# One remainder step of the angle changes places with k's product with the decay, from unit 3 on

## The chip, the cores and the metric

The kernel runs on one core of a Trainium2 chip. The metric is the device time of one execution in microseconds. A core has five engines that work side by side, each through its own instructions in order: TensorE (PE, with its weight loads as PEld), VectorE (DVE), ScalarE (ACT), GpSimd (POOL) and SyncE (SP), of which SP here only issues DMAs.

## The reference

An attention block with complex gates is followed by a gated feed-forward block. Sizes: 4 batches, 8 heads, 768 steps of time, head width 48; 3072 tokens, model width 384, inner width 1024.

```python
scale = np.minimum(mag, 0.999) / (mag + 1e-06)      # mag = |a_re + i a_im|
...
for t in range(S):
    new_re = ar * S_re - ai * S_im
    new_im = ar * S_im + ai * S_re
    S_re, S_im = (new_re + kv, new_im)              # kv = outer product of k and v at t
    y[:, :, t] = np.einsum('bhd,bhde->bhe', q[:, :, t], S_re)
...
h = ((x @ w1) * (x @ w2)) @ w3
return h @ w_out                                    # x is y with the heads side by side
```

## The kernel before

**Units.** A unit is half of one batch's time: 384 steps of all 8 heads, so there are 8 units, 0 to 7. The channels lie as 3 column tiles of 384 steps on 128 partitions. The recurrence is not stepped: the gates are brought to a running decay and a running angle, k and q are multiplied by decay (or its inverse), cosine and sine, and then scores, states and outputs are matrix products (lines 997 to 1081). Behind a unit's outputs come the feed-forward products of that unit, w1 and w2 (lines 1083 to 1136, `m` in the trace) and the fused w3 times w_out (lines 1178 to 1193, `o`).

**Feed-forward products from unit 3 on.** Each of the 16 column blocks of w1 and w2 takes a first product of six matmuls (called h0, h1, ... in the prediction), a copy of its PSUM tile in place by ScalarE (L1125), and a correction of three matmuls onto the same tile (d0, d1, ...). An even correction is followed by a copy to `ab` by ScalarE (L1132), an odd one by a product into `ab` by VectorE (L1107). There are four PSUM banks for them (`ps_m`), and the order on TensorE is h0, h1, h2, d0, h3, d1, h4, d2, and so on. So h4 takes the bank of h0, once the copy behind d0 has ended. Each `o` product is cut into two halves of eight matmuls; ScalarE copies the result behind the second (L1190). Of the products of unit u - 1 some stand ahead of the transposes, scores and outputs of unit u, and the last of them, two halves or three of the `o` products, behind them.

**Gates.** While TensorE works on the products of unit u - 1, VectorE and ScalarE prepare unit u in `gates_apart` (lines 624 to 769), in two parts: part 0 is column tile 0 (128x384), part 1 is tiles 1 and 2 (128x768). A step on a part has its number behind its name. The steps that matter here, in the order of the program:
- `ang_0`, `ang_1` (L687, VectorE): running sums of the angle, one per tile; `turns_0`, `turns_1` (L691, ScalarE): the whole turns in it as integers; a small copy of the angles (L692, VectorE).
- `k_0`, `k_1` (`scaled`, L703, VectorE): k times the inverse decay. It needs k from memory.
- `z5_0` (L709, VectorE): the angle of tile 0 less its whole turns; `abs_0`, `cos_0` (L711, L713, ScalarE); then `z5_1`, `abs_1`, `cos_1`.
- `q_0`, `q_1` (L717, VectorE), `sin_0`, `sin_1` (L723, ScalarE), the end columns (L729, ScalarE, three small copies).
- `kc`, `qc`, `ks`, `qs` (L749, L752, L757, L763, VectorE): k and q times cosine and sine, each followed by DMAs on SP's queue that lay the tiles out for the scores (L739), and at last the DMAs of V (L592).

ScalarE's steps that go through the helper `act` all bear L637 in the trace. k, q and V of unit u + 1 are loaded by GpSimd's queue (L528, L570) when the outputs of unit u have been written, behind the last GpSimd step of these outputs (L1053).

**Who sets the order.** TensorE's order is a list written ahead (`unit`, `pieces`, `ffn`). The order of all other engines comes from a planner that runs while the program is built (`run`, lines 1576 to 1737): it keeps a clock per engine from the costs written in `TIMES` and in the `yield`s, and behind every item of TensorE's list it takes the next gate step if that step can start before TensorE is through the next item (`fits`, `fill`). Gate steps are taken strictly in the order of the generator; the next is looked at only when the one before has been placed. So a gate step's place in its engine's queue is a place between the copies of two products. A ScalarE step of n tiles is written as 0.2 + 0.325 n, a VectorE one as 0.06 + 0.475 n, a first product as 1.05, a correction as 0.53, a half as 2.58, a hand-over as 0.15; a copy behind a product as 0.48 on ScalarE and 0.56 on VectorE.

```python
bound = clock["PE"] + sum(d for kind, _ in seq[k + 1:k + 2] for e, d in TIMES[kind] if e == "PE")
slack = EARLY if k < heads[0] else LATE if gate["u"] <= held["unit"] else SLACK
return start(op) < bound and start(op) + op[1] <= request(op[0], k) + slack
```

k's landing is due in the plan at the end of the outputs plus 1.1 (GpSimd's last step), 0.7 (issue), 1.8 and 2.4 (transfer) and 0.2 (lines 560 to 563, 1724).

Of the kernel before, what the change touches and what calls it, by code (L numbers as in the profile page):

```python
# [378 lines left out]
def kernel(  # L379
# [244 lines left out]
    def gates_apart(u, A, Z):  # L624
# [7 lines left out]
        def on(e, name, i, *after):  # L632
            n = (1, KD - 1)[i]
            return e, (0.2 + 0.325 * n if e == "ACT" else 0.06 + 0.475 * n), (name, i), after

        def act(**kw):
            chain(nc.scalar.activation(**kw))  # L637
# [61 lines left out]
        def scaled():  # L699
            for i, s in parts:  # L700
                yield on("DVE", "k_", i, ("r2_", i), ("k", u))
                k = g["k"][:, :, 0:TT]
                tt(out=k[:, s], in0=k[:, s], in1=r[:, s], op=OP.mult)  # L703

        if u > 2:
            yield from scaled()
        for i, s in parts:
            yield on("DVE", "z5_", i, ("turns_", i))
            stt(out=Z[:, s], in0=re[:, s].bitcast(I32), scalar=-2 * PI, in1=Z[:, s], op0=OP.mult, op1=OP.add)  # L709
            yield on("ACT", "abs_", i, ("z5_", i))  # L710
            act(out=re[:, s], in_=Z[:, s], func=AF.Abs)  # L711
            yield on("ACT", "cos_", i, ("abs_", i))
            act(out=re[:, s], in_=re[:, s], func=AF.Sin, scale=-1.0, bias=QUARTER)  # L713
# [57 lines left out]
    def gates(u, split):  # L771
# [18 lines left out]
        if u > 1:  # L790
            yield from gates_apart(u, A, Z)
            return
# [1051 lines left out]
```

## Time and profile before

| | us |
|---|---|
| median of 3 runs | 538.68 |
| lowest and highest run | 535.29, 539.11 |
| the profiled execution | 539.2 |
| its span in the profile | 537.4 |

The profile is that of one execution. Its span reaches from the first instruction to the last; 1.8 us of the execution lie around it. A timeline row has the start, the time, the engine and line, what is written from what, the shape and the count, and in brackets the engine's idle time just before with what ended it. A row of waits has the sum, the count and the longest. PE rows of the products overlap each other by some tenths, since matmuls are pipelined.

### The profile page before, as it was taken

The page shows a single profiled execution, that of the slowest core. Times are in us where ns is not written, and L with a number is a line of the kernel's source. Part 1 is how long each engine was busy: PE and PEld are TensorE (multiplying, and loading weights), DVE is VectorE, ACT ScalarE, POOL GpSimd, SP SyncE. Part 2 cuts the span into 40 slices and gives each one's busy share as a digit, 9 for nine tenths or more (in the row PEclk, how much of TensorE's full clock was granted, in tenths as well). Part 3 has the DMA queues.
Part 4 walks back from the last instruction along what each step waited for, and adds up shares of the span by engine and source line. Part 5 has one row for each costly group of instructions (what it writes and reads, how often), then busy time and mean ns, then how long its engine had stood idle before and what let it go on. Part 6 is the DMA issues. An engine that isn't in the chain of part 4 may idle for free.

```text
span 537.4 us, 13665 instructions
## 1 busy us (share of the span) xinstructions
PE 498.4 (93%) x5594; PEld 377.7 (70%) x5594; DVE 374.0 (70%) x607; ACT 336.8 (63%) x569; POOL 247.1 (46%) x311
## 2 busy tenths in 40 slices
PE   4689889999998999999999999999999999999995
PEld 2355565556755678967888678867996788878972
DVE  6999697856769977866873776578657846336660
ACT  6979867485575556884788457855797555213420
POOL 1000000017868866830675565576458458335510
PEclk9899899999999999999999999999999999999999
DMA  8999966874178616494569437972797166935511
GB/s 249 367 395 280 189 200 176 227 171 111 40 204 212 116 57 187 116 224 80 141 195 224 93 77 204 227 138 63 197 214 135 46 176 167 213 95 187 194 56 37
DMA packets 66520, 89.75 MB, mean 167 GB/s; under 512 B 29968, under 2 KB 53968, under 8 KB 65680
## 3 DMA queue, kind: packets, MB, share of 16 engines
q1 hardware_dynamic: 58016, 59.15, 44.0%
q0 software_dynamic: 8432, 29.63, 20.2%
q8 instruction: 46, 0.75, 0.6%
q14 instruction: 26, 0.21, 0.1%
HBM read 61.60 MB, written 4.72 MB: 123 GB/s over the span
## 4 chain that ended last, share of the span: by engine, by line
PE 48%; DVE 16%; DMA 16%; issue 6%; ACT 5%; POOL 5%; SPq 2%; POOLq 0%; DVEq 0%; ACTq 0%
PE m L1091 21%; PE o L1186 16%; PE y L1045 5%; PE sc L1006 4%; DMA k<-in_k_dram 3%; DMA V<-vr 2%; DMA QL<-gA 2%; DMA KL<-k 2%; DVE gA L752 2%; DVE gR L749 2%; DMA q<-in_q_dram 1%; DMA look<-in_a_re_dram 1%; PE kv L1071 1%; DMA raw<-in_w_dram 1%; DMA KL<-gR 1%
## 5 line engine op out<-in xcount | busy, mean ns | idle before, releaser
L1186 PE MATMUL o<-w3o,ab 128*128 128x384 f32 x384 | 131.5, 492 | 0.0
L1091 PE MATMUL m<-x,low 128*128 128x384 f32 x576 | 119.2, 339 | 0.0
L1091 PEld LDWEIGHTS m<-x,low 128*128 128x128 f32 x576 | 102.6, 188 | 0.2 <-ACT m L1125 0.2
L1186 PEld LDWEIGHTS o<-w3o,ab 128*128 128x128 f32 x384 | 70.5, 190 | 45.5 <-issue 2.2
L1107 DVE TENSOR_TENSOR ab<-m,ab 128x384 f32<-128x384 f32 x64 | 35.0, 554 | 59.3 <-PE m L1091 43.9
L1091 PE MATMUL m<-x,wh 128*128 128x384 f32 x288 | 69.8, 351 | 3.5 <-ACT ab L1132 2.5
L1125 ACT ACTIVATE m<-m 128x384 f32<-128x384 f32 x96 | 45.5, 475 | 32.7 <-PE m L1091 31.2
L1091 PE MATMUL m<-xT,ws 128*128 128x384 f32 x192 | 63.1, 487 | 1.2 <-ACT xT L1056 1.2
L1091 PEld LDWEIGHTS m<-x,wh 128*128 128x128 f32 x288 | 50.7, 188 | 7.9 <-ACT ab L1132 3.8
L1327 POOL TENSOR_SCALAR look<-look 128x192 f32<-128x192 f32 (+1 forms) x54 | 53.8, 996 | 4.9
L1091 PEld LDWEIGHTS m<-xT,ws 128*128 128x128 f32 x192 | 36.0, 190 | 25.6 <-ACT xT L1056 1.7
L1272 POOL MEMSET seen<- 128x256 bf16 x1 | 0.3, 316 | 111.8 <-DVE ab L1107 111.8
L1324 POOL TENSOR_TENSOR look<-look 128x256 f32<-128x256 f32 (+1 forms) x42 | 30.6, 730 | 43.5 <-DMA look<-in_w_dram 24.3
L1009 DVE COPY_PREDICATED A<-mask,sc 128x512 f32<-128x512 uint8 x48 | 32.8, 732 | 23.4 <-PE sc L1006 23.3
L1053 POOL TENSOR_TENSOR x<-x,x 128x384 fp32r<-128x384 f32 x18 | 22.2, 1233 | 54.4 <-DVE x L1052 54.4
L1288 POOL TENSOR_TENSOR seen<-seen,look 128x192 bf16<-128x192 bf16 (+1 forms) x54 | 43.3, 803 | 4.4
L1190 ACT COPY ot<-o 128x384 f32<-128x384 f32 x24 | 11.5, 478 | 50.5 <-PE o L1186 50.2
L1045 PE MATMUL y<-A,V 128*32 128x128 f32 x768 | 40.7, 273 | 2.5 <-issue 2.4
L994 ACT COPY KT<-tp 128x384 f32<-128x384 f32 x40 | 34.3, 867 | 6.8 <-PE tp L992 6.4
L1045 PEld LDWEIGHTS y<-A,V 128*32 128x32 f32 x768 | 34.9, 110 | 3.7 <-issue 3.2
L1006 PEld LDWEIGHTS sc<-QL,KL 96*32 96x32 f32 x1536 | 28.5, 110 | 10.3 <-issue 3.6
L1045 PE MATMUL y<-QL,T 96*32 96x128 f32 x640 | 35.3, 272 | 0.0
(163 smaller groups left out, 916.4 us busy)
## 6 DMA issues: line engine op xcount, KB each, us to landing
looked<-in_w_dram POOLq DMA_DIRECT2D x15, 512.0 KB, 4.6
look<-in_w_dram POOLq DMA_DIRECT2D x26, 256.0 KB, 4.0
raw<-in_w_dram SPq DMA_DIRECT2D x6, 1024.0 KB, 10.3
KL<-gR SPq DMA_DIRECT2D x24, 192.5 KB, 3.1
KL<-k SPq DMA_DIRECT2D x24, 192.5 KB, 7.0
QL<-gA SPq DMA_DIRECT2D x24, 192.0 KB, 9.0
QL<-q SPq DMA_DIRECT2D x24, 192.0 KB, 7.5
raw<-in_w_dram SPq DMA_DIRECT2D x6, 768.0 KB, 7.4
```

Of the source, the lines that this page charges most:

```text
L994: nc.scalar.copy(out=KT_t[u, c][:, :, :, x].rearrange("p h d f -> p f d h"), in_=tp.rearrange("p f (d h) -> p f d h", h=H))
L1006: nc.tensor.matmul(out=sc[SB * g:SB * g + SB, j, s0:C], lhsT=KL[:, x * n + j, w][:, s0:s0 + SB], rhs=QL[:, x * n + j, w][:, s0:C], start=T ...
L1009: last["sc", u, c, x] = nc.vector.copy_predicated(out=A[:, x * n:(x + 1) * n], data=sc, mask=mask)
L1045: nc.tensor.matmul(out=o, lhsT=a, rhs=b, start=s0, stop=s1)
L1053: nc.gpsimd.tensor_tensor(out=x[2], in0=x[1], in1=x[0], op=OP.subtract)
L1091: nc.tensor.matmul(out=out, lhsT=a, rhs=b, start=start and i == 0, stop=i == len(terms) - 1, skip_group_check=not start)
L1107: last["ab", u, j] = nc.vector.tensor_tensor(out=ab_t[u][:, j], in0=m, in1=ab_t[u][:, j], op=OP.mult)
L1125: nc.scalar.activation(out=got[m], in_=got[m], func=AF.Copy, scale=1.0 + 1.0 / BITS)
L1186: nc.tensor.matmul(out=m, lhsT=ab_t[u][:, f, t * P:(t + 1) * P], rhs=w3o[:, f], start=(f == 0), stop=(f == KF - 1))
L1288: nc.gpsimd.tensor_tensor(out=seen[:, 0:n], in0=seen[:, 0:n], in1=x, op=OP.add)
L1324: tt(out=x, in0=x, in1=x, op=OP.mult)
L1327: ts(out=x, in0=x, scalar1=low, scalar2=None, op0=OP.is_ge)
```

## The change

In units 3 to 7 the two instructions of `scaled` (k_0, k_1) are emitted behind the first remainder step z5_0 instead of ahead of it. The order on VectorE was k_0, k_1, z5_0, z5_1 and is written as z5_0, k_0, k_1, z5_1. In the generator abs_0 and cos_0 follow k_1 as before. Units 0 to 2 are not touched.

```diff
-        if u > 2:
-            yield from scaled()
         for i, s in parts:
             yield on("DVE", "z5_", i, ("turns_", i))
             stt(out=Z[:, s], in0=re[:, s].bitcast(I32), scalar=-2 * PI, in1=Z[:, s], op0=OP.mult, op1=OP.add)
+            if u > 2 and i == 0:
+                yield from scaled()
             yield on("ACT", "abs_", i, ("z5_", i))
             act(out=re[:, s], in_=Z[:, s], func=AF.Abs)
             yield on("ACT", "cos_", i, ("abs_", i))
```

## Rows read from the trace of the kernel before

**Rows 1.** The page's first part: busy us, share and count by engine.
```profile
PE 498.4 (93%) x5594; PEld 377.7 (70%) x5594; DVE 374.0 (70%) x607; ACT 336.8 (63%) x569; POOL 247.1 (46%) x311
```

**Rows 2.** Waits of PE over the span: who for whom, sum, times, longest.
```profile
PE m L1091 <- ACT ab L1132: 2.5, 3, 0.9
...
PE sc L1006 <- DMA V<-vr: 1.3, 1, 1.3
PE tp L992 <- DVE k L757: 1.2, 2, 0.7
...
PE m L1091 <- DVE ab L1107: 0.9, 3, 0.4
PE tp L992 <- DVE gR L749: 0.7, 3, 0.3
```

**Rows 3.** Busy time by window: width, then PE, PEld, DVE, ACT, POOL, clock, DMA.
```profile
318.00:345.00 27.00, 25.11 (x180) 22.90 (x180) 18.29 (x24) 21.11 (x40) 18.05 (x23) 1.00 0.80 206
...
430.00:462.00 32.00, 30.56 (x207) 27.42 (x206) 15.76 (x23) 18.64 (x37) 21.70 (x29) 1.00 0.73 183
462.00:537.00 75.00, 69.12 (x684) 54.08 (x682) 33.54 (x84) 16.68 (x36) 26.26 (x31) 1.00 0.41 123
```

**Rows 4.** Timeline of VectorE, gates of unit 7.
```profile
430.08 0.79 DVE L692 COPY st_ang<-gZ 128x9 f32<-128x9 f32 x1
436.55 1.43 DVE L703 TENSOR_TENSOR k<-k,gR 128x384 f32<-128x384 f32 x2 [5.68 <-DMA k<-in_k_dram]
437.89 1.43 DVE L709 SCALAR_TENSOR_TENSOR gZ<-re,gZ 128x384 f32<-128x384 int32 x2
...
446.71 0.55 DVE L749 TENSOR_TENSOR gR<-k,re 128x384 f32<-128x384 f32 x1
```

**Rows 5.** Timeline of ScalarE, gates of unit 7.
```profile
426.28 0.51 ACT L637 ACTIVATE re<-gZ 128x384 int32<-128x384 f32 x1
...
438.55 0.52 ACT L637 ACTIVATE re<-gZ 128x384 f32<-128x384 f32 x1 [1.45 <-DVE gZ L709]
438.98 0.46 ACT L1132 COPY ab<-m 128x384 f32<-128x384 f32 x1
...
439.85 0.48 ACT L1125 ACTIVATE m<-m 128x384 f32<-128x384 f32 x1
440.26 0.83 ACT L637 ACTIVATE re<-gZ 128x768 f32<-128x768 f32 x1
...
441.77 0.94 ACT L637 ACTIVATE re<-re,consts 128x768 f32<-128x768 f32 x1
```

**Rows 6.** Timeline of TensorE, units 5, 6 and 7.
```profile
325.73 0.79 PE L1091 MATMUL m<-x,wh 128*128 128x384 f32 x3 [0.82 <-ACT ab L1132]
...
382.44 0.79 PE L1091 MATMUL m<-x,wh 128*128 128x384 f32 x3 [0.85 <-ACT ab L1132]
...
427.49 0.49 PE L1045 MATMUL y<-QL,T 96*32 96x128 f32 x7
...
439.49 0.79 PE L1091 MATMUL m<-x,wh 128*128 128x384 f32 x3 [0.85 <-ACT ab L1132]
...
442.78 0.69 PE L1091 MATMUL m<-x,wh 128*128 128x384 f32 x3
```

**Rows 7.** VectorE from 300 to 450 us by form: count, busy us, mean ns.
```profile
L709 DVE SCALAR_TENSOR_TENSOR gZ<-re,gZ 128x768 f32<-128x768 int32 x3 | 2.9, 955 | 0.0
...
L709 DVE SCALAR_TENSOR_TENSOR gZ<-re,gZ 128x384 f32<-128x384 int32 x3 | 1.7, 554 | 0.0
```

**Rows 8.** Timeline of VectorE, units 3 to 6.
```profile
216.62 1.03 DVE L709 SCALAR_TENSOR_TENSOR gZ<-re,gZ 128x384 f32<-128x384 int32 x1
...
265.73 1.43 DVE L703 TENSOR_TENSOR k<-k,gR 128x384 f32<-128x384 f32 x2
...
322.85 1.43 DVE L703 TENSOR_TENSOR k<-k,gR 128x384 f32<-128x384 f32 x2 [1.13 <-DMA k<-in_k_dram]
...
377.53 1.43 DVE L703 TENSOR_TENSOR k<-k,gR 128x384 f32<-128x384 f32 x2 [1.88 <-DMA k<-in_k_dram]
```

## The prediction

> **What bounds the kernel now.** I read the page's first part, then TensorE's waits, then the busy time by stage, then the timelines of VectorE, ScalarE and TensorE around the gates of each unit from 3 on. TensorE is busy for 498.4 of 537.4 us [rows 1]: it is the bound, its order is fixed, and the change adds nothing to it and takes nothing from it. So the change is worth what it alters in TensorE's waits. From the first gates of unit 3 to the end these are few. The five groups of [rows 2] are 2.5, 1.3, 1.2, 0.9 and 0.7 us, together 6.6: the correction's copy (L1132) with three waits, V's transfer, the transposes that wait for k times sine or for k times cosine, and VectorE's products. No gain can be larger than this sum. By stage the gaps are 27.00 - 25.11 = 1.89 us in the gates of unit 5 and 32.00 - 30.56 = 1.44 in those of unit 7 [rows 3]; unit 6 has one wait of 0.85 [rows 6]. The last 75 us hold 5.9 [rows 3], about as much as the tail behind the last product needs, so a microsecond won earlier should reach the end.
>
> The three long waits have one pattern, seen best in unit 7. VectorE is done with the angle's sums and the small copy behind them at 430.87, then stands for 5.68 us until k has landed; k times decay runs from 436.55 to 437.98, and only behind it come the two remainders L709 (z5_0, z5_1) [rows 4]. ScalarE has put the turns of tile 0 down at 426.79, so z5_0 had had its input for 11 us when it started. ScalarE stands 1.45 us at the absolute value abs_0, which wants z5_0, and the correction's copy L1132 that stands behind abs_0 comes at 438.98 [rows 5]. TensorE waits for that copy for 0.85 us, until 439.49, because its fifth first product needs the PSUM bank that the copy frees; units 5 and 6 show the same with 0.82 and 0.85 [rows 6].
>
> **The change, part by part.** Nothing is added or removed: per unit one instruction of 128x384 passes two. DMA issues, SP's and POOL's queues and TensorE's order stay as they are written; what can move with them is where the planner puts the gates' later steps.
>
> *The moved instruction.* z5_0 costs 0.554 us, z5_1 0.955 [rows 7]. In units 5, 6 and 7 VectorE waits 1.13, 1.88 and 5.68 us for k [rows 4, 8], and z5_0 fits into each of these: it costs nothing there, and k's product starts when it did. If that cover were gone it would cost 0.55 us on VectorE. In units 3 and 4 VectorE doesn't wait for k (the product starts without a wait at 265.73 in unit 4) [rows 8], so there the two merely change places and z5_1 ends when it did: gain 0. From both sides: z5_0 at 1.03 (its longest, in unit 3 [rows 8]) against 0.55 could lose 0.5 us per unit, and an earlier abs_0 could win the wait for V behind unit 3, 1.3 us. I take 0, because the rest of both chains stands where it stood.
>
> The row first: z5_0 of unit 3 took 1.03 us where those of units 5 to 7 took 0.554 [rows 7, 8]. The Trainium skill, SBUF — State Buffer, section Who interferes with whom, says that a VectorE instruction with two SBUF inputs contends with a GpSimd instruction that reads SBUF, and that whichever issued later is blocked throughout. By it z5_0 of unit 5, which now starts amid GpSimd's checks, may take the longer time; the sum would be some 0.1 us less, as it would still end before k lands.
>
> *The stall that goes.* With z5_0 done before k lands, abs_0 waits for nothing. In unit 7 the copy L1132 can then run as soon as its product is there, and the 0.85 us go. What is late next is z5_1. It stands right behind k's product: 437.98 + 0.955 less some 0.1 of overlap gives 438.85, 0.3 us later than abs_0 started before (438.55 [rows 5]). So abs_1 becomes the instruction at which ScalarE stands, and all hangs on what is queued behind it.
>
> *What stands behind abs_1.* The planner decides by the costs written in the kernel; I use them for the order alone. I set its TensorE clock to 0 at the end of the last output of the unit before. Two output halves end at 5.16, then the first products h0, h1, h2 at 6.21, 7.26, 8.31, the correction d0 at 8.84, h3 at 9.89, d1 at 10.42, h4 at 11.47. k is due at 1.1 + 0.7 + 1.8 + 2.4 + 0.2 = 6.2, on VectorE it is multiplied by 7.74, z5_0 by 8.28, and abs_0 may start at 8.43: that falls behind h2's copy and ahead of d0's copy, which is where [rows 5] show it. The same walk also gives the places of cos_0, abs_1, cos_1, both sines and the end columns in the trace of before, so I trust it for after. With the change abs_0 goes behind h0's copy, cos_0 behind h1's, and abs_1 is due at 7.74 + 1.01 + 0.15 = 8.90: too late for the place ahead of d0's copy (limit 8.84), so it goes behind it and ahead of h3's. The copy that TensorE waits for is free. The end columns go from behind d5 to behind d3, and k times cosine with them, two pairs of products or about 3.2 us earlier (446.71 before [rows 4]).
>
> *Unit 5.* The same places hold, and the cosine and sine products come earlier by more than the small waits of the transposes and of L1107. All gaps of this stage go: 1.89, I take 1.9; from below 1.0, if one pair's lateness stays.
>
> *Unit 7.* abs_1 starts at 438.9. From [rows 5] a step on ScalarE costs its duration less some 0.1 of overlap: abs_1 0.73, h3's copy 0.38, cos_1 0.84, h4's copy 0.38, sin_0 0.42, d2's copy 0.36, which ends about 442.0. TensorE wants the bank that d2's copy frees at 439.49 - 0.85 + 3.2 = 441.85 (h4 to h6 is 439.49 to 442.78 [rows 6], less a slow first tile). That leaves 0.15, with the hand-over 0.3, as a new small stall. Gain 1.44 - 0.3 = 1.1.
>
> *Unit 6.* Here three halves come first, so abs_1 lands behind h0's copy and ahead of h1's, that is ahead of d0's copy too. k's product starts at 377.53 [rows 8], z5_1 ends at 377.53 + 1.43 + 0.87 = 379.83; abs_1 0.73, two copies of 0.38 and d0's 0.36 end at 381.7; TensorE begins to wait at 382.44 - 0.85 = 381.59 [rows 6]. Gain about 0.6. If the planner also puts cos_1 (0.84) ahead of d0's copy, which a few hundredths of its clock decide, the copy ends at 382.5 and 0.2 is lost. I take the middle, 0.2.
>
> *Sum.* 0 + 0 + 1.9 + 0.2 + 1.1 = 3.2 us. The profiled execution took 539.2 us, its span of 537.4 and 1.8 around it; 539.2 - 3.2 = 536.0. It lies 0.5 above the median of 538.68, so from the median I predict 535.5, 0.6% less. A measurement of this kernel can tell about 1% (5.4 us) from no change, so this would count as within it.
>
> **The rivals.**
> *A. The stall is handed on and the time stays:* abs_0 is early, but each microsecond comes back at abs_1, and the later steps keep their slots. For it: z5_1 ends as late as before, and k lands 2.4 us later than the planner thinks (436.55 is 8.6 us behind the last output's end at 427.98 [rows 4, 6], the plan has 6.2). Against it: behind h3's copy nothing urgent stands. Time 538.7, gain 0 to 1.
>
> *B. Slower: abs_1 stands ahead of d0's copy in all three units.* The point from which it decides is the planner's 8.84 for units 5 and 7; 0.06 us less in its clock is enough. Price: ScalarE goes on at z5_1's end, so d0's copy ends at z5_1's end + 0.73 + 0.36, in unit 7 at 440.0, and TensorE starts at 440.05 instead of 439.49: 0.56 worse. Unit 5 the same, unit 6 0.2: 538.7 + 1.3 = 540.0. For it: the margin is thin. Against it: the walk meets before's order everywhere.
> The Trainium skill, TensorE: Matmul & The Clock Gate, section Architectural detail: the array is 16× 32×32, not 1× 128×128, has ScalarE and VectorE as strict FIFO queues; by this rule a ready copy can't pass a waiting abs_1, and the time would be this rival's 540.0. The trace agrees that none passes: L1132 waited behind abs_0.
>
> *C. More is won:* the earlier cosine products also free the transposes of unit 4 and V's transfer behind unit 3. For it: these waits are 6.6 us in all [rows 2]. Against it: units 3 and 4 gain nothing by the steps above. 6.6 at most, 532.1.
>
> *D. The change does not do what it says:* z5_0 waits for the turns and holds k's product up. Against it: they were done long before [rows 5]. Price 0.5 a unit, 2.5: 541.2.
>
> **How the numbers follow.** Forecast (gain 2 to 4.3) 0.55; A 0.17; B 0.08; C (gain 4.3 to 6.6) 0.17; D 0.03. The range leaves out B, D and the end of C, and takes in A: 532.4 to 538.9. Faster by over 1% (under 533.3) is most of C: 0.15. Slower by over 1% (over 544.1) is beyond all priced cases: 0.03. Within 1%: 0.82.
>
> **What would show it.** Right: in units 5 to 7 z5_0 runs ahead of the wait for k, and L1132 no longer ends a TensorE wait in units 5 and 7; ScalarE's wait for L709 is now at abs_1 with 128x768; the cosine products of units 5 and 7 start 2 to 4 us earlier; the windows of units 5 and 7 lose 1 to 2 us of gaps. Wrong: the correction's copy still ends waits of 0.8 us or more in unit 5 or 7, cosine products in their old slots, or new waits of TensorE in stages where there were none.

## The result: slower, and the profile after

| | before | after |
|---|---|---|
| median of 20 runs each, us | 537.28 | 544.51 |
| the profiled execution, its span, us | 539.2, 537.4 | 546.09, 544.3 |
| ratio of the times, 95% interval | | 1.0138, 1.0115 to 1.0160 |

The changed kernel is 1.4% slower; 535.5 was forecast, with a chance of 0.03 for slower by over 1%. The page's first part and its slices of TensorE's granted clock, after (a digit is a fortieth of the span, in tenths of full speed):

```profile
PE 501.8 (92%) x5594; PEld 381.3 (70%) x5594; DVE 375.3 (69%) x607; ACT 335.5 (62%) x569; POOL 245.0 (45%) x311
...
PEclk9899899999999999999999999999889999999999
```

The same instructions, but TensorE is busy for 3.4 us more than in [rows 1], and the clock has a dip in the slices 29 and 30, about 381 to 408 us, where none was. To find the place, I cut TensorE's timeline at the end of the last output of each unit (a unit's stretch is then the feed-forward products of the unit before, with this unit's gates beside them, and its own scores and outputs):

| unit | before | after | difference | forecast |
|---|---|---|---|---|
| 3 | 56.47 | 58.61 | +2.14 | 0 |
| 4 | 57.24 | 57.18 | -0.06 | 0 |
| 5 | 54.11 | 54.41 | +0.30 | -1.9 |
| 6 | 59.63 | 67.30 | +7.67 | -0.2 |
| 7 | 53.94 | 51.94 | -2.00 | -1.1 |

With -0.86 ahead of unit 3 and -0.3 behind unit 7 that is the 6.9 us between the spans. All of it, and more, sits in unit 6. The same cut is used on the runs below. In one of their profiles, that of the change without unit 6 (e1_not6), the clock also dipped in unit 3, behind a wait of 1.52 us for V's transfer. A ratio leaves out the slow executions of a kernel (over 1.5% longer than its fastest), a median does not; the profiles of e1_not6, e2_only6 and e8_only7 are of slow ones, which are late already where unit 3 begins (205.5 to 206.8 us, before 200.5).

TensorE's waits over the span, after (who for whom, sum, times, longest):

```profile
PE m L1091 <- DVE ab L1107: 5.4, 6, 1.8
...
PE m L1091 <- ACT ab L1132: 3.5, 2, 3.2
PE sc L1006 <- DMA V<-vr: 1.6, 1, 1.6
```

Against [rows 2]: the wait for the correction's copy L1132 comes twice instead of three times, but one of the two is 3.2 us; the wait for VectorE's products L1107 has grown from 0.9 to 5.4. TensorE's timeline in units 3, 5, 6 and 7, after:

```profile
218.84 0.79 PE L1091 MATMUL m<-x,wh 128*128 128x384 f32 x3 [0.55 <-DVE ab L1107]
...
335.67 0.79 PE L1091 MATMUL m<-x,wh 128*128 128x384 f32 x3 [1.62 <-DVE ab L1107]
...
389.64 1.33 PE L1091 MATMUL m<-x,wh 128*128 128x384 f32 x3 [3.23 <-ACT ab L1132]
390.77 2.12 PE L1091 MATMUL m<-x,low 128*128 128x384 f32 x6
...
402.79 1.05 PE L1091 MATMUL m<-x,wh 128*128 128x384 f32 x3 [1.84 <-DVE ab L1107]
403.64 2.12 PE L1091 MATMUL m<-x,low 128*128 128x384 f32 x6
...
451.25 0.79 PE L1091 MATMUL m<-x,wh 128*128 128x384 f32 x3 [0.26 <-ACT ab L1132]
```

Unit 6 has two long waits, and right behind each of them six matmuls take 2.12 us. In the trace of before such six took 1.21 behind the wait of 0.85 in [rows 6]:

```profile
383.07 1.21 PE L1091 MATMUL m<-x,low 128*128 128x384 f32 x6
```

Busy time by window, after (width, then PE, PEld, DVE, ACT, POOL, clock, DMA share, GB/s):

```profile
318.00:345.00 27.00, 24.89 (x179) 22.77 (x178) 20.27 (x25) 19.89 (x39) 16.31 (x21) 1.00 0.85 210
...
372.00:402.00 30.00, 25.16 (x118) 21.44 (x116) 17.95 (x23) 19.36 (x37) 22.03 (x32) 0.94 0.61 158
...
390.00:395.00 5.00, 5.00 (x22) 5.00 (x22) 0.54 (x2) 2.95 (x9) 4.25 (x8) 0.71 0.26 73
395.00:400.00 5.00, 4.52 (x28) 4.22 (x27) 5.00 (x7) 4.05 (x7) 4.21 (x6) 1.00 0.48 133
400.00:405.00 5.00, 3.08 (x13) 2.53 (x13) 2.74 (x4) 3.31 (x6) 3.06 (x5) 0.81 0.96 206
405.00:410.00 5.00, 5.00 (x70) 4.68 (x69) 1.15 (x3) 2.98 (x6) 2.35 (x4) 0.84 1.09 237
...
402.00:430.00 28.00, 27.20 (x394) 22.02 (x395) 16.43 (x29) 18.37 (x32) 11.79 (x17) 0.94 0.67 143
```

and the same two long windows of before:

```profile
372.00:402.00 30.00, 29.15 (x200) 26.28 (x199) 17.97 (x26) 23.44 (x44) 16.91 (x24) 1.00 0.86 203
...
402.00:430.00 28.00, 27.46 (x514) 20.10 (x513) 22.06 (x34) 17.38 (x28) 17.40 (x22) 1.00 0.45 95
```

So the granted clock, 1.00 in both stretches before (the 2.4 GHz level), falls part of the time to the 1.2 GHz level: 0.71 in the window behind the first wait (0.50 from 389.6 to 392.8 us taken alone), 1.00 again from 395, 0.81 and 0.84 in the two windows with the second wait and what follows it. The 7.67 us of unit 6 come out as follows. Waits of TensorE of 0.2 us and more there: before 0.85 + 0.48 = 1.33, after 3.23 + 0.48 + 1.84 = 5.55, so 4.2 more. The rest, 3.45, is the slow clock: 58 us at 0.94 instead of 1.00 make 58 x 0.06 = 3.5.

The Trainium skill, TensorE: Matmul & The Clock Gate, section What's actually happening, says that a clock gate halves TensorE's clock when it has been idle. The trace agrees in the direction: each of the two dips stands behind a wait. Not every wait has one: behind the 1.62 us in unit 5 the clock stays at 1.00 (the window from 318 to 345 us).

What held ScalarE up? Its timeline in units 6 and 7, after:

```profile
381.27 0.85 ACT L637 ACTIVATE re<-gZ 128x768 f32<-128x768 f32 x1 [0.31 <-DVE gZ L707]
...
382.43 0.47 ACT L1132 COPY ab<-m 128x384 f32<-128x384 f32 x1
...
383.21 0.92 ACT L637 ACTIVATE re<-re,consts 128x768 f32<-128x768 f32 x1
387.46 1.25 ACT L596 ACTIVATE gA<-re,consts 128x1152 f32<-128x1152 f32 x1 [3.33 <-issue]
...
388.71 0.47 ACT L1125 ACTIVATE m<-m 128x384 f32<-128x384 f32 x1
389.12 0.47 ACT L1132 COPY ab<-m 128x384 f32<-128x384 f32 x1
...
447.93 0.85 ACT L637 ACTIVATE re<-gZ 128x768 f32<-128x768 f32 x1 [1.21 <-DVE gZ L707]
```

Up to 384.1 it goes as the better branch of the forecast has it: abs_1 waits 0.31, d0's copy at 382.43 is in time. Then comes an instruction that the prediction doesn't mention: L596, the first step of the *next* unit's gate head, a check of the sign of unit 7's `re`. It stands for 3.33 us, and behind it the copies L1125 and L1132 for which TensorE waits. The bracket names no DMA ("issue"), but the load of `re` does, by what writes that tile from 370 to 400 us:

```profile
L528 SPq DMA_DIRECT2D re<-in_a_re_dram x1: 588/588/588, 376.9 to 376.9; - x1
...
DMA to landing us min/median/max: 10.5/10.5/10.5
```

376.9 + 10.5 = 387.4: L596 starts when its input has landed. Before, it stood behind the end columns (L729), late enough:

```profile
386.35 0.20 ACT L729 COPY st_dec<-gA 128x3 f32<-128x3 f32 x1
...
387.88 1.27 ACT L596 ACTIVATE gA<-re,consts 128x1152 f32<-128x1152 f32 x1
```

The planner's rule makes the reason plausible; a run below tests it. Besides the gate generator it has a list `others`, in which the next unit's head waits; when the head of the gate generator doesn't want ScalarE, a step of `others` that fits may take the place. With the change cos_1 is placed earlier, the generator's next step is q_0 on VectorE, and ScalarE has a gap in the plan. The plan has `re` landing 0.63 (issue) + 1.8 + 2.4 + 0.2 = 5.0 us behind its issue; the trace says 10.5. VectorE's timeline, after, for the smaller changes, with one row of GpSimd's:

```profile
214.39 0.56 DVE L707 SCALAR_TENSOR_TENSOR gZ<-re,gZ 128x384 f32<-128x384 int32 x1
...
216.70 1.62 DVE L707 SCALAR_TENSOR_TENSOR gZ<-re,gZ 128x768 f32<-128x768 int32 x1
216.87 0.62 POOL L1324 TENSOR_TENSOR look<-look 128x256 f32<-128x256 f32 x1
218.24 0.54 DVE L1107 TENSOR_TENSOR ab<-m,ab 128x384 f32<-128x384 f32 x1
...
267.51 0.56 DVE L707 SCALAR_TENSOR_TENSOR gZ<-re,gZ 128x384 f32<-128x384 int32 x1 [0.47 <-ACT re L637]
...
323.04 0.56 DVE L707 SCALAR_TENSOR_TENSOR gZ<-re,gZ 128x384 f32<-128x384 int32 x1
...
331.69 0.56 DVE L752 TENSOR_TENSOR gA<-q,re 128x384 f32<-128x384 f32 x1 [1.28 <-ACT st_dec L729]
...
335.07 0.55 DVE L1107 TENSOR_TENSOR ab<-m,ab 128x384 f32<-128x384 f32 x1
...
377.28 0.74 DVE L707 SCALAR_TENSOR_TENSOR gZ<-re,gZ 128x384 f32<-128x384 int32 x1
378.94 1.43 DVE L703 TENSOR_TENSOR k<-k,gR 128x384 f32<-128x384 f32 x2 [0.93 <-DMA k<-in_k_dram]
...
400.39 1.89 DVE L763 TENSOR_TENSOR q<-q,gZ 128x384 f32<-128x384 f32 x2
402.19 0.54 DVE L1107 TENSOR_TENSOR ab<-m,ab 128x384 f32<-128x384 f32 x1
...
440.09 0.56 DVE L707 SCALAR_TENSOR_TENSOR gZ<-re,gZ 128x384 f32<-128x384 int32 x1
445.60 1.43 DVE L703 TENSOR_TENSOR k<-k,gR 128x384 f32<-128x384 f32 x2 [4.95 <-DMA k<-in_k_dram]
...
451.70 0.55 DVE L749 TENSOR_TENSOR gR<-k,re 128x384 f32<-128x384 f32 x1
```

z5_0 stands ahead of k's product in all units, as written, and ahead of a wait for k in units 5, 6 and 7 (in unit 5 the wait is 0.31 us). In unit 4 it stands still itself, for 0.47 us, until ScalarE has the turns. In unit 3 z5_1 has got ahead of the product L1107 that TensorE wants at 218.84, and it takes 1.62 us there instead of the 0.955 of [rows 7]; GpSimd's check L1324, 0.62 us long, runs within it. In unit 5 the cosine products (L749, L752) start so early that the first qc waits 1.28 us for the end columns, which read the tile that it overwrites (`gA`), and the L1107 behind them is late: that is TensorE's 1.62 at 335.67. In unit 6 everything behind ScalarE's stall is late on VectorE too: L1107 at 402.19 stands behind the sine products, the wait of 1.84.

### The profile page after: what moved, and what is told of

Same layout as the page of the kernel before. It is cut to its first block, busy times and chain, and to the rows that moved or that the text cites. A ratio compares the mean times of both kernels' runs of the same rounds, so it can differ in the third digit from the quotient of the medians.

```text
span 544.3 us, 13662 instructions
## 1 busy us (share of the span) xinstructions
PE 501.8 (92%) x5594; PEld 381.3 (70%) x5594; DVE 375.3 (69%) x607; ACT 335.5 (62%) x569; POOL 245.0 (45%) x311
## 4 chain that ended last, share of the span: by engine, by line
PE 52%; DVE 16%; DMA 11%; issue 7%; ACT 7%; POOL 5%; SPq 2%; POOLq 0%; DVEq 0%; ACTq 0%
PE m L1091 24%; PE o L1186 16%; PE y L1045 5%; PE sc L1006 5%; DMA k<-in_k_dram 2%; PE kv L1071 2%; DVE gA L752 2%; DVE gR L749 2%; DMA QL<-gA 1%; DMA look<-in_a_re_dram 1%; DMA q<-in_q_dram 1%; DVE q L763 1%; DVE ab L1107 1%; DVE k L757 1%; DMA re<-in_a_re_dram 1%
## 5 line engine op out<-in xcount | busy, mean ns | idle before, releaser
L1091 PE MATMUL m<-x,low 128*128 128x384 f32 x576 | 121.0, 343 | 0.3 <-ACT m L1125 0.3
L1091 PEld LDWEIGHTS m<-x,low 128*128 128x128 f32 x576 | 104.4, 191 | 0.6 <-ACT m L1125 0.6
L1091 PE MATMUL m<-x,wh 128*128 128x384 f32 x288 | 71.1, 356 | 8.9 <-DVE ab L1107 5.4
L1107 DVE TENSOR_TENSOR ab<-m,ab 128x384 f32<-128x384 f32 x64 | 35.2, 553 | 62.7 <-PE m L1091 39.1
L1125 ACT ACTIVATE m<-m 128x384 f32<-128x384 f32 x96 | 45.8, 478 | 39.6 <-PE m L1091 39.0
L1091 PEld LDWEIGHTS m<-x,wh 128*128 128x128 f32 x288 | 51.8, 192 | 13.3 <-DVE ab L1107 7.1
L1324 POOL TENSOR_TENSOR look<-look 128x256 f32<-128x256 f32 (+1 forms) x42 | 29.7, 708 | 40.9 <-DMA look<-in_w_dram 24.6
L1190 ACT COPY ot<-o 128x384 f32<-128x384 f32 x24 | 11.5, 478 | 52.5 <-PE o L1186 52.2
L994 ACT COPY KT<-tp 128x384 f32<-128x384 f32 x40 | 34.1, 869 | 3.8 <-PE tp L992 3.6
## 6 DMA issues: line engine op xcount, KB each, us to landing
look<-in_w_dram POOLq DMA_DIRECT2D x26, 256.0 KB, 4.4
```

What stands on the lines that cost most here:

```text
L994: nc.scalar.copy(out=KT_t[u, c][:, :, :, x].rearrange("p h d f -> p f d h"), in_=tp.rearrange("p f (d h) -> p f d h", h=H))
L1091: nc.tensor.matmul(out=out, lhsT=a, rhs=b, start=start and i == 0, stop=i == len(terms) - 1, skip_group_check=not start)
L1107: last["ab", u, j] = nc.vector.tensor_tensor(out=ab_t[u][:, j], in0=m, in1=ab_t[u][:, j], op=OP.mult)
L1125: nc.scalar.activation(out=got[m], in_=got[m], func=AF.Copy, scale=1.0 + 1.0 / BITS)
L1324: tt(out=x, in0=x, in1=x, op=OP.mult)
```

## The experiments

Theory: the loss is L596 in ScalarE's queue, ahead of its data, and what TensorE's clock makes of the wait. Rival: the loss is spread over the units, since every gate's second half starts later (abs_1 behind k). The table has each kernel's stretches by unit, from one profile each; the ratio is that of the times to runs of the kernel before on the same chip, with its interval. Two kernels were profiled twice (e3_hold and e10_hold, e5_due and e11_due): their stretches lie up to 0.13 and 0.59 us apart, so a few tenths in this table mean nothing.

| kernel | 3 | 4 | 5 | 6 | 7 | ratio (95%) |
|---|---|---|---|---|---|---|
| before | 56.47 | 57.24 | 54.11 | 59.63 | 53.94 | |
| after | 58.61 | 57.18 | 54.41 | 67.30 | 51.94 | 1.0138 (1.0115 to 1.0160) |
| e1_not6 | 58.55 | 57.18 | 54.42 | 59.24 | 51.71 | 0.9952 (0.9915 to 0.9988) |
| e2_only6 | 57.07 | 57.20 | 54.51 | 67.55 | 53.62 | 1.0114 (1.0026 to 1.0202) |
| e3_hold | 57.32 | 57.19 | 54.43 | 58.13 | 51.76 | 0.9939 (0.9895 to 0.9984) |
| e4_before_hold | 57.43 | 57.27 | 55.07 | 59.20 | 53.00 | 1.0002 (0.9952 to 1.0051) |
| e5_due | 57.30 | 56.79 | 52.50 | 59.28 | 52.79 | 0.9966 (0.9932 to 0.9999) |
| e6_dose3 | 57.89 | 57.19 | 54.43 | 64.59 | 51.72 | 1.0107 (1.0067 to 1.0147) |
| e7_dose1 | 57.42 | 57.21 | 53.69 | 59.60 | 51.82 | 1.0025 (0.9988 to 1.0061) |
| e8_only7 | 56.35 | 57.23 | 54.41 | 59.65 | 52.68 | 0.9984 (0.9946 to 1.0021) |
| e9_kdue | 57.87 | 57.23 | 54.87 | 57.91 | 52.24 | 0.9953 (0.9910 to 0.9996) |
| e10_hold | 57.43 | 57.19 | 54.45 | 58.00 | 51.67 | 0.9964 (0.9924 to 1.0004) |
| e11_due | 57.08 | 57.24 | 53.09 | 59.62 | 52.79 | 0.9986 (0.9948 to 1.0025) |

### The change without unit 6, and in unit 6 alone

Diff against the kernel after; for the second, `(6,)` in both places.

```diff
+        if u > 2 and u not in (3, 4, 5, 7):
+            yield from scaled()
         for i, s in parts:
...
-            if u > 2 and i == 0:
+            if u in (3, 4, 5, 7) and i == 0:
                 yield from scaled()
```

> The change in units 3, 4, 5 and 7; unit 6 keeps before's order. Theory (the loss sits in unit 6, where the next unit's sign check L596 was queued on ScalarE behind cos_1 and waits there for a DMA): the 7.7 us of unit 6 go, about 537 us, ratio to before 0.995 to 1.002, no wait of TensorE above 1 us in unit 6 and the granted clock of its stretch back at 1.00. Rival (the loss is spread, the slower start of each gate being the cause): only about a fifth of the 6.9 us goes, 543 us, ratio 1.010.

> The change in unit 6 alone. Theory (the loss sits in unit 6): the 7.7 us stand by themselves, about 545 us, ratio 1.012 to 1.017, with ScalarE's wait of some 3 us at L596, TensorE's wait for L1132 behind it, and a granted clock under 0.96 in unit 6. Rival (spread loss): some 1.5 us, ratio 1.003.

Without unit 6: 537.63 us, ratio 0.9952, unit 6 back at 59.24, its longest wait 0.76. In unit 6 alone: 546.84, ratio 1.0114, unit 6 at 67.55 with a wait of 3.97 for the copy and one of 1.73 for VectorE's product. Both as the theory has them. The first ratio also stands against the rival's 1.010. That of the second doesn't decide: its interval, from few executions, is nearly 1% to each side and just takes in the rival's 1.003, so there the stretch and its waits speak for the theory. The two don't quite add up (0.66% together, 1.38% measured), which that interval allows.

### The next unit's head held back

Diff in `gate_head`, against the kernel after; the control has the same two lines in the kernel before.

```diff
         A = g["A"] = slot(u, "A", "gA")[:, :, 0:TT]
+        if u > 3 and not g["go"]:
+            yield None
         for f in range(2):
             yield "ACT", 1.45, "low", (("re", u),)
```

> The whole change, and from unit 4 on the gate steps of the next unit (its sign check L596 among them) are held back until the step that the unit before it has reached its second half. Theory (L596 in ScalarE's queue, not the moved instruction, makes the loss of unit 6): the 3.2 us wait and the lower clock of unit 6 go, 537 us or less, ratio 0.990 to 1.002. Rival (the later second absolute value holds ScalarE up by itself): the wait for L1132 in unit 6 stays at 2 to 3 us, 543 to 545 us, ratio 1.010 to 1.015.

> The kernel before with the same hold and nothing else: the control for the run with the hold. Both theories: the sign check came behind the end columns already, so the hold moves it little: within 1.5 us of before, ratio 0.997 to 1.003.

537.08 us, 0.9939; the control 537.57, 1.0002. The moved instruction is where it was, abs_1 still waits (0.27 in unit 6), and yet unit 6 takes 58.13 instead of 67.30 and has one TensorE wait of 0.48. The hold by itself changes nothing in the time. That is the theory's result; a late abs_1 costs TensorE nothing in this unit. The transfer is no faster either: `re` was again 10.6 us on its way. It is the place of L596 that matters.

### The planner's idea of the landing

```diff
             load_gates(u + 1, ("re",), (("ang_", 1),))
+            if u > 2:
+                ready["re", u + 1] += 5.0
```

> The whole change, with nothing held back; only the time at which the planner believes the next unit's sigmoid input re to have landed is set 5 us later (units 4 to 7), near to when the trace shows it. Theory (the planner put L596 into a gap that by its own numbers was free, because it has re landing 5 us too early): L596 moves behind the end columns by itself, the wait of 3.2 us and the lower clock of unit 6 go, 535 to 537.5 us, ratio 0.991 to 0.999. Rival (a wrong due time is not the cause, the earlier cosine fills ScalarE anyway): unit 6 keeps a TensorE wait of 2 us or more, ratio over 1.008.

ScalarE's timeline in unit 6 of this kernel:

```profile
386.79 0.20 ACT L733 COPY st_dec<-gA 128x3 f32<-128x3 f32 x1
...
388.38 1.26 ACT L596 ACTIVATE gA<-re,consts 128x1152 f32<-128x1152 f32 x1
```

L596 has gone behind the end columns by itself, with no wait; 536.1 us, 0.9966. So the due time that the plan had for `re` decides, as the theory says. This run shows that the due time is enough, not that the plan's other numbers are right. Unit 6 itself gains little by it (59.28, and 59.62 in e11_due, against 59.63): its transposes wait 0.6 us for VectorE's sine products instead.

### The stall without the load

Against the kernel with the hold; `range(1 ...)` for the smaller dose.

```diff
             act(out=re[:, s], in_=re[:, s], func=AF.Sin, scale=-1.0, bias=QUARTER)
+            for _ in range(3 if (u, i) == (6, 1) else 0):
+                act(out=re[:, s], in_=Z[:, s], func=AF.Abs)
+                act(out=re[:, s], in_=re[:, s], func=AF.Sin, scale=-1.0, bias=QUARTER)
```

> The kernel with the hold, which has no TensorE wait at L1132 in unit 6; there, behind cos_1 of tile 1, the pair of absolute value and cosine is done three times more (same values, the planner doesn't know of it): 3 x 1.6 = 4.7 us of ScalarE at the place where L596 stood for 4.3. No DMA is waited for. Theory (a held ScalarE queue is enough: the wait at L1132 and the fall of the clock follow from it): a TensorE wait of 3 to 4 us in unit 6, the granted clock under 0.97 behind it, unit 6 6 to 9 us longer than with the hold alone, ratio 1.006 to 1.013. Rival (the clock fell for another reason, by chance of that run): the wait alone, 3 to 4 us longer, clock 1.00.

> The same with the pair done once more: 1.6 us of ScalarE. Theory (the loss has a threshold: ScalarE has about 1 us to spare there, and a short wait of TensorE doesn't lower the clock): a TensorE wait of about 0.5 us, clock 1.00, unit 6 up to 1 us longer than with the hold, ratio 0.994 to 0.998. Rival (the loss goes with the dose): a third of the 6 to 9 us, 2 to 3 us longer, ratio 0.998 to 1.000.

TensorE's timeline with three pairs:

```profile
391.03 1.33 PE L1098 MATMUL m<-x,wh 128*128 128x384 f32 x3 [4.52 <-ACT ab L1139]
392.15 2.12 PE L1098 MATMUL m<-x,low 128*128 128x384 f32 x6
```

and the windows of it:

```profile
384.00:394.00 10.00, 5.48 (x24) 5.16 (x23) 3.92 (x6) 8.68 (x16) 7.97 (x12) 0.81 0.46 119
394.00:404.00 10.00, 10.00 (x53) 9.93 (x53) 5.82 (x8) 7.92 (x14) 8.81 (x12) 0.85 0.93 223
```

A TensorE wait of 4.52, the same 2.12 behind it, the clock at 0.81 and 0.85: a held ScalarE queue is enough, with no load in it, and the time is 1.0107. Against the hold alone unit 6 is 64.59 - 58.13 = 6.5 longer; the waits explain 4.52 - 0.48 = 4.0 of it, which leaves 2.4 for the clock. With one pair:

```profile
382.46 0.79 PE L1098 MATMUL m<-x,wh 128*128 128x384 f32 x3 [0.56 <-ACT ab L1139]
386.73 0.79 PE L1098 MATMUL m<-x,wh 128*128 128x384 f32 x3 [0.83 <-ACT ab L1139]
```

The second of these waits is the dose (the first belongs to an abs_1 that waited 1.03 in this execution, 0.76 more than with the hold alone), the clock stays at 1.00, and unit 6 is 1.5 us longer, between the theory's 1 at most and the rival's 2 to 3. The clock's half of the theory holds. The time is not as the theory has it: 1.0025, where 0.994 to 0.998 stood, and the rival's 0.998 to 1.000 lies in its interval. What makes its runs slower than its profile tells stays open.

### Unit 7 alone

The first diff with `(7,)`.

> The change in unit 7 alone, which has no next unit whose head could fill a gap. Theory (the mechanism of the forecast is right where nothing else gets in): unit 7 is 1.9 us shorter than before (53.9), the waits for L1132 there under 0.4 us in all, and the time 0.3 to 0.4% less: ratio 0.995 to 0.998. Rival (the gain of unit 7 in the changed kernel came from the rest of unit 6, whose late end gave k time to land): unit 7 within 0.5 us of before, ratio 0.999 to 1.001.

Unit 7 takes 52.68, 1.3 less than before, with waits of 0.17 for the copy and 0.33 for VectorE's product; 0.9984. This lies between the two, and the interval of the ratio takes in both. The stretch is the better witness: unit 7 took 53.00 to 53.94 in the three kernels without the change there and 51.67 to 52.79 in the ten with it, 1.4 less by the means. So the gain is there, nearer to the 1.1 that was forecast than to the 2.0 of the changed kernel. In the kernels with the change in the other units too, and no due time moved, unit 7 took 51.7 to 51.9; where those other 0.7 to 1.0 come from I didn't take apart.

### The landing of k, and the two repaired kernels again

Against the kernel with the hold, in the due time of what GpSimd's queue loads:

```diff
-        ready[name] = clock["DMA"] + 0.2
+        ready[name] = clock["DMA"] + (2.6 if name[0] == "k" and name[1] > 4 else 0.2)
```

> The whole change with the hold, and k believed to land 2.4 us later from unit 5 on, as the trace shows it, so that the steps behind k's product are planned where they can run. Theory (what is left of the loss in unit 5 comes from steps planned too early for k: kc and qc stand ahead of a product that TensorE waits 1.6 us for): that wait goes under 0.5 us, unit 5 is 1 to 2 us shorter than the 54.4 with the hold alone, ratio 0.988 to 0.994. Rival (the places behind k don't matter any more once L596 is out of the way): unit 5 at 54 or more, ratio 0.993 to 0.998.

> The kernel with the hold once more, beside the others on one chip. If the 0.6% that it was faster than before is real: ratio 0.991 to 0.997 again. If it was the luck of few executions: 0.997 to 1.002.

> The kernel with the later due time of re once more, beside the others on one chip. If it differs from the one with the hold (0.9966 against 0.9939 so far, on two chips), it is again 0.2 to 0.4% slower than that; if not, both within 0.2%.

TensorE's waits in unit 5 with k's later due time:

```profile
337.14 0.44 PE L996 MATMUL tp<-ident,k 128*128 128x128 f32 x2 [0.74 <-DVE k L761]
339.42 0.79 PE L1095 MATMUL m<-x,wh 128*128 128x384 f32 x3 [0.26 <-DVE ab L1111]
353.53 1.32 PE L1010 MATMUL sc<-QL,KL 96*32 96x128 f32 x64 [1.26 <-DMA V<-vr]
```

The wait of 1.62 for VectorE's product is gone, as the theory had it, but unit 5 takes 54.87: the transposes wait again, and the scores wait 1.26 for V's transfer. 0.9953 is the rival's number. What one wait gave up in unit 5 was taken by others.

The kernel with the hold came out at 0.9964 beside the 0.9939 of its first run, the one with the later due time at 0.9986 beside 0.9966. The order is the same twice, inside the intervals. So the kernel with the hold is some 1.8% faster than the changed one (0.9939 and 0.9964 over 1.0138: 0.980, 0.983), and perhaps half a per cent faster than the one before: one interval ends below 1, the other at 1.0004.

## Why the prediction was wrong

**The step that failed** stands where the cost of the change is set out: "what can move with them is where the planner puts the gates' later steps". I walked the planner along the one generator that was changed and took the rest of ScalarE's queue as it stood. But the planner fills gaps from a second list, and the order of that list hangs on the first. In unit 6 it put L596 at a place where its data were 3.3 us away. Consequently the sum for unit 6 was -0.2 and measured +7.67, and the sentence "Slower by over 1% (over 544.1) is beyond all priced cases" was true only because no case had a foreign instruction in the queue. With L596 out of the way the total comes out near the forecast: 0.994 to 0.996 of the time of before, against 535.5/538.68 = 0.994. That is luck in part. By the stretches of the two runs of the kernel with the hold, against the one profile of before, units 6 and 7 gave some 1.6 and 2.2 us (forecast 0.2 and 1.1) and so made up for unit 5, which gave nothing (forecast 1.9), and unit 3, which lost some 0.9 (forecast 0).

**A second omission** is TensorE's clock. All cases priced a wait of TensorE at its length. The waits of 3.23 and 1.84, 4.2 us more of waiting than before, cost 7.67, since part of the products that followed ran at the lower level.

Point by point:
- *The moved instruction is free.* Right where it was to count: z5_0 ends before k lands in units 5 to 7, and k's product starts when k is there. The price that I weighed for it, the blocked VectorE of the Trainium skill (SBUF — State Buffer, Who interferes with whom), did not fall on z5_0: it took 0.56 us in units 3, 4, 5 and 7 and 0.74 in unit 6, never the 1.03 of [rows 8]. In unit 3 the longer time went to z5_1, 0.67 us more than in [rows 7], with GpSimd's 0.62 us within it; that these two belong together is likely by their size, no run separates them.
- *The stall at L1132 goes; abs_1 is late next.* Right in all three units, as far as the unit's own steps go: the wait is gone in unit 5, 0.26 in unit 7 (forecast 0.3), and ScalarE's wait for the remainder is now at the 128x768 form, 0.31 and 1.21.
- *Unit 6, by its own steps.* d0's copy was in time, with abs_1 ahead of it: the better of the two branches (abs_1 stood behind h1's copy, one place later than the walk had it). With L596 held back unit 6 gains 59.63 - 58.13 = 1.5 (1.6 in e10_hold), more than the 0.6 of that branch.
- *Unit 5, gain 1.9.* Wrong, 0 by the profiles: 54.4 in five with the change, 54.1 to 55.1 in the four without it (with the change 54.9 in e9_kdue and less in three: 53.7 in e7_dose1, 52.5 and 53.1 in the kernel with the later due time of `re`, which I didn't take apart). The stall at L1132 went, and a wait of 1.62 for L1107 came, behind cosine products that had moved ahead of it. Rival A, the stall handed on, is what happened here, though not at abs_1, where that rival had it, and not with the later steps in their old places. The claim "all gaps of this stage go" failed: I counted what the earlier products free, and not what they now stand ahead of.
- *Unit 7, gain 1.1.* Right, and more: 2.0 in the changed kernel, 1.3 alone, 1.4 by the means of all profiles. The first cosine product came 6.1 us behind k's product (451.70 - 445.60) instead of 10.2 in [rows 4].
- *Unit 3, gain 0.* Nearly right. Its +2.14 is mostly that one profile: the stretch took 56.35 to 57.43, mean 56.8, in the four profiles without the change there, and 57.1 to 57.9, mean 57.5, in the seven others with it and an even clock. So the change costs some 0.6 here. The nearest cause is TensorE's wait for the L1107 behind z5_1, 0.55 in the changed kernel and at most 0.66 in the others. It goes with z5_1's time: 0.23 at most in the four profiles where z5_1 took 1.37 us or less, 0.45 to 0.66 in the five where it took 1.61 or more. The forecast had 0.5 as its lower bound, for a long z5_0: the right kind of price on the wrong instruction.
- *Rival B*, abs_1 ahead of d0's copy, had 540.0 and 0.08. It named the right engine and the right kind of wait, but the wrong instruction: with the hold abs_1 stands in that place in unit 6 and costs nothing. The strict order of ScalarE's queue, cited there from the Trainium skill, is what the trace shows: the copy L1125 could not pass the waiting L596.
- *Rival C.* No: the waits of [rows 2] didn't go as a whole. Their 6.6 us were not all of TensorE's waits either: its waits for the copies L994 are missing, 0.99, 0.47 and 0.48 us in units 3, 4 and 6 of the kernel before.
- *Rival D.* In unit 4 alone, and without a cost: z5_0 waited 0.47 us for the turns there and held k's product up, which started 9.70 us behind the last output of the unit before instead of 8.73, but the stretch stayed at 57.18 (57.24 before). That the turns were done long before had been read from unit 7. In the other units z5_0 waited for nothing.

## What to carry to other kernels

When a planner sets the order, a change to one stream moves the others too: walk every list from which it may fill a gap, and compare the landing that it believes in for each load with the one that the trace shows. An instruction that waits for a transfer belongs behind everything on its engine for which TensorE is waiting. And a wait of the bounding engine is to be priced with what its clock does afterwards, when it is longer than the waits that this stage had before: here 0.85 us cost its length, 3.23 and 4.52 cost more.

## What the runs showed of the hardware

A wait of 3 to 4.5 us of TensorE made the next six matmuls take 2.12 us instead of 1.23, with a granted clock of 0.71 to 0.85 in the windows behind it, and so cost 1.6 to 1.8 times its length (6.5 for 4.0 more of waiting with three pairs, 7.67 for 4.2 in the changed kernel); the waits of 0.56 and 0.83 of the smaller dose left it at 1.00. In between there are both: behind 1.52 us in unit 3 of e1_not6 the clock fell (0.50 from 252.7 to 256.0 us), behind 1.62 us in unit 5 of the changed kernel it did not. A load of 576 KB, whose median is 9.0 us in the changed kernel, took 10.5 us from issue to landing while loads of k, q and V of the same size, issued 2.2 to 3.8 us ahead of it, were under way. Issued 3.1 us later behind the last output of the unit before (e5_due), it took 6.7 us and so landed 16.9 us behind that output instead of 17.5. Nothing in the bracket of the instruction that waited for it said so: there the profile has only "issue"; in e2_only6, where L596 stood for 4.04 us in the same place, the bracket names another load.
